# Linear attention ahead of two expert layers: q (k^T v) taken head by head from two row halves

## The chip, the core and the metric

One NeuronCore of a Trainium2 chip runs the whole program. The metric is device time in microseconds (us) of one execution; each figure for the kernel before is from runs of the same program. The engines are named as in the profile: PE (TensorE, matrix products; its weight loads are PEld), ACT (ScalarE), DVE (VectorE), POOL (GpSimd), and SP, whose queue issues most transfers.

## The reference

The inputs are float32: q, k, v of 4 batches x 8 heads x 576 tokens x 64, and the weights of two feed-forward stages.

```python
kv  = einsum('bhsd,bhse->bhde', k, v)
out = einsum('bhsd,bhde->bhse', q, kv)
x   = out / sqrt(mean(out*out, -1) + 1e-6) * g_norm        # RMS norm per token and head
x   = x.transpose(0, 2, 1, 3).reshape(2304, 512)
h   = x @ w_in;  x = (h * clip(h + 3, 0, 6) / 6) @ w_out   # 512 -> 2048 -> 512
p   = domain_probs / (domain_probs.sum(-1) + 1e-9)         # 2304 x 4
out = sum over e of p[:, e] * (relu(x @ w1[e]) @ w2[e])    # 4 experts, 512 -> 1024 -> 512
```

## The kernel before

**Three stages.** The attention stage works through 8 half batches (4 heads each, numbered i). The first feed-forward stage (`ff_in`, `ff_out`) multiplies in three products of split float32 halves. The expert stage does the same in `quad` and `outs`. PE holds 128 x 128 weights at a time; a float32 product appears in the trace as two PE instructions, each with its own weight load, so 10 products are 20 rows' worth of instructions.

**One step of attention.** The loop over i overlaps three half batches: in step i, `att_q(i)` and `att_kv(i)` run, then `att_out(i-1)`, then `att_x(i-2)`.

- `att_q` transposes q by products with the identity (64 x 64 pieces in the four quarters of PE; tile `pq`; the ninth slice goes into the bank `kvp`), and ACT copies the result to `qT` (lines 217 and 219).
- `att_kv` accumulates k^T v for 4 heads, also in quarters (line 229), and ACT copies each head's 64 x 64 block to its place in `kvbd` (line 234, four instructions). `kvbd` holds two heads as a 128 x 128 block-diagonal matrix, zero elsewhere.
- `att_out` multiplies 128 tokens of `qT` with `kvbd` for a pair of heads (line 247): five tiles of tokens (the fifth, odd one has 64 tokens), two pairs of heads, 10 products into three banks `po` (two tiles, two tiles, the odd one). Bank after bank, ACT squares (line 253) and DVE sums over 64 values (line 256).
- `att_rms`: DVE forms mean + 1e-6 (`va`), ACT takes the root (line 279), DVE takes the reciprocal and a Newton step of four instructions (lines 281 to 286), then scales the three banks into `xt` (line 269).
- `att_x` transposes `xt` (line 305) into three banks `px`; ACT scales by g_norm and rounds to the high half (line 315, "hi"), DVE forms the low half (line 316, "lo").

**Order and banks.** PSUM has 8 banks: two for `pq` and `ph`, six (`psb` with 5 and `psc` with 1) for everything else. The order written in the loop is a priority, not the final order: at compile time a planner places each engine's instructions by its own estimate of when they are ready, and may pull later work forward into a gap. On the chip each engine then runs its own list in that fixed order, waiting where it must. So pieces of the weight conversion (`convert`, lines 142 to 160; three ACT and seven DVE instructions for half a weight tile) stand between the steps of attention. The four `ff_in` products that can start early (`EARLY`) are called by `fill()` in the last three steps. The transfers of q, k and v wait in SP's queue for one of seven buffers.

Of the kernel before, what the change touches and what calls it, by code (L numbers as in the profile page):

```python
# [17 lines left out]
def kernel(  # L18
# [63 lines left out]
    psb = ctx.enter_context(tc.tile_pool(name="psb", bufs=5, space=bass.MemoryType.PSUM))  # L82
    psc = ctx.enter_context(tc.tile_pool(name="psc", bufs=1, space=bass.MemoryType.PSUM))

    turn = [0]

    def bank_b(shape, name):
        turn[0] += 1
        pool, tag = (psc, "c") if turn[0] % 6 == 0 else (psb, "b")
        return pool.tile(shape, F32, tag=tag, name=name)  # L90
# [9 lines left out]
    kvbd = [const.tile([P, NP, P], F32, name=f"kvbd{i}") for i in range(2)]  # L100
    ssq = const.tile([P, 5, HH], F32, name="ssq")
# [10 lines left out]
    todo = [(n, h) for n in range(len(ftiles)) for h in range(2)]  # L112

# [16 lines left out]
    def convert(n):  # L130
# [5 lines left out]
        for h in range(2):  # L136
# [24 lines left out]
            load_raw()  # L161
# [7 lines left out]
    def att_load(i):  # L169
        b, hf = divmod(i, 2)  # L170
        t = {}
        for nm, src in (("q", q), ("k", k), ("v", v)):
            m = natile[0] % 7
            natile[0] += 1
            pool, tag = (accp, "acc") if m < 5 else (wp, f"w{m - 1}")
            t[nm] = pool.tile([P, NP, CJ, D], F32, tag=tag, name=f"{nm}in")
            nc.sync.dma_start(
                out=t[nm].rearrange("p r j d -> p r (j d)"),
                in_=src[b, hf * HH:(hf + 1) * HH].rearrange("(r x) (s j) d -> (x s) r (j d)", x=2, j=CJ),
            )  # L180
        st[i] = t
# [6 lines left out]
    def banks(b):  # L188
        c = cut(b)
        w128 = [(o, P) for o in range(0, c - P + 1, P)]  # L190
        rest = c - len(w128) * P
        odd = [(c - rest, rest)] if rest else []
        w128 += [(o, P) for o in range(c, S - P + 1, P)]
        end = c + (S - c) // P * P
        odd += [(end, S - end)] if end < S else []
        assert len(w128) == 4 and odd == [(odd[0][0], D)]
        return [tuple(w128[:2]), tuple(w128[2:]), tuple(odd)]

    half = [slice(x * D, (x + 1) * D) for x in range(2)]

    def att_q(i):

        t = st[i]
        t["qT"] = qTs = wp.tile([P, NP, S], F32, tag=f"w{i % 2}", name="qT")
        qv = qTs.rearrange("p r (s j) -> p r s j", j=CJ)
        pq = [psa.tile([P, CB, CP], F32, tag="a", name="pq") for _ in range(NP)]
        t["kvp"] = kvp = [bank_b([P, 2, D], "kvp") for _ in range(NP)]
        for j in range(CJ):  # L210
            for x in range(2):
                for r in range(NP):
                    to = pq[r][half[x ^ r], j, :] if j < CB else kvp[r][half[x ^ r], 1, :]
                    nc.tensor.matmul(  # L214
                        to, lhsT=t["q"][half[x], r, j, :], rhs=ident[half[x], half[x]], start=True, stop=True)
        for r in range(NP):
            nc.scalar.activation(out=qv[:, r, :, :CB], in_=pq[r].rearrange("p j s -> p s j"), func=AF.Copy)  # L217
        for r in range(NP):
            nc.scalar.activation(out=qv[:, r, :, CB], in_=kvp[r][:, 1, :], func=AF.Copy)

    def att_kv(i):
# [3 lines left out]
        kvp = t["kvp"]  # L225
        for j in range(CJ):
            for x in range(2):
                for r in range(NP):
                    nc.tensor.matmul(  # L229
                        kvp[r][half[x ^ r], 0, :], lhsT=t["k"][half[x], r, j, :], rhs=t["v"][half[x], r, j, :],  # L230
                        start=(j == 0), stop=(j == CJ - 1))
# [5 lines left out]
    def att_out(i):  # L237
# [3 lines left out]
        t["xt"] = xt = wp.tile([P, 3, 2, HH, D], F32, tag=f"w{2 + i % 2}", name="xt")  # L241
        t["po"] = []
        for tt in banks(b):
            po = psb.tile([P, 2, NP, P], F32, tag="b", name="po")
            for m, (o, w) in enumerate(tt):
# [4 lines left out]
            t["po"].append(po)  # L250
        for g, tt in enumerate(banks(b)):
            w, nm = tt[0][1], len(tt)
            nc.scalar.activation(
                out=xt[:w, g, :nm].rearrange("p m h d -> p m (h d)"),
                in_=t["po"][g][:w, :nm].rearrange("p m r e -> p m (r e)"), func=AF.Square)
            nc.vector.tensor_reduce(  # L256
                out=ssq[:w, 2 * g:2 * g + nm, :], in_=xt[:w, g, :nm], axis=AX.X, op=ALU.add)

    def att_rms(i):


        b, hf = divmod(i, 2)
        t = st[i]
        va, r0, w1_, ri = (sp.tile([P, 5, HH], F32, tag=n, name=n) for n in ("va", "r0", "nw", "ri"))

        def scale():
            for g, tt in enumerate(banks(b)):
                w, nm = tt[0][1], len(tt)
                nc.vector.tensor_tensor(
                    out=t["xt"][:w, g, :nm].rearrange("p m h d -> p (m h) d"),  # L270
                    in0=t["po"][g][:w, :nm].rearrange("p m r (h d) -> p (m r h) d", d=D),
                    in1=ri[:w, 2 * g:2 * g + nm, :].rearrange("p m h -> p (m h)").unsqueeze(2).to_broadcast(
                        [w, nm * HH, D]),
                    op=ALU.mult)

        return [
            lambda: nc.vector.tensor_scalar(
                out=va, in0=ssq, scalar1=1.0 / D, scalar2=1e-6, op0=ALU.mult, op1=ALU.add),
            lambda: nc.scalar.activation(out=r0, in_=va, func=AF.Sqrt),
            lambda: nc.vector.reciprocal(out=r0, in_=r0),  # L280
            lambda: nc.vector.scalar_tensor_tensor(
                out=w1_, in0=va, scalar=FMAX, in1=r0, op0=ALU.min, op1=ALU.mult),
            lambda: nc.vector.tensor_tensor(out=w1_, in0=w1_, in1=r0, op=ALU.mult),
            lambda: nc.vector.tensor_scalar(
                out=w1_, in0=w1_, scalar1=-0.5, scalar2=1.5, op0=ALU.mult, op1=ALU.add),
            lambda: nc.vector.tensor_tensor(out=ri, in0=w1_, in1=r0, op=ALU.mult),
            scale,
        ]

    def att_x(i):  # L290

        b, hf = divmod(i, 2)
        t = st.pop(i)
# [483 lines left out]
```

## Time and profile before

| | |
|---|---|
| median of 3 runs | 1234.51 us (1234.01 to 1236.36) |
| the profiled execution, own time | 1233.99 us |
| its span, first to last instruction | 1232.2 us |
| PE busy | 1212.6 us (98%) |
| DVE, ACT busy | 760.4 us, 531.3 us |
| granted PE clock, mean | 0.997 |
| attention's last "lo" (line 316) | starts 98.9 us into the span |

The shares are averages over stages. PE is without a gap from about 73 us to nearly the end; the gaps lie ahead of that, in the attention stage. All of the changed lines act within the first 100 us.

### The profile page before, as it was taken

The page shows a single profiled execution, that of the slowest core. Times are in us where ns is not written, and L with a number is a line of the kernel's source. Part 1 is how long each engine was busy: PE and PEld are TensorE (multiplying, and loading weights), DVE is VectorE, ACT ScalarE, POOL GpSimd, SP SyncE. Part 2 cuts the span into 40 slices and gives each one's busy share as a digit, 9 for nine tenths or more (in the row PEclk, how much of TensorE's full clock was granted, in tenths as well). Part 3 has the DMA queues.
Part 4 walks back from the last instruction along what each step waited for, and adds up shares of the span by engine and source line. Part 5 has one row for each costly group of instructions (what it writes and reads, how often), then busy time and mean ns, then how long its engine had stood idle before and what let it go on. Part 6 is the DMA issues. An engine that isn't in the chain of part 4 may idle for free.

```text
span 1232.2 us, 17425 instructions
## 1 busy us (share of the span) xinstructions
PE 1212.6 (98%) x7069; PEld 1064.8 (86%) x7069; DVE 760.4 (62%) x1457; ACT 531.3 (43%) x1050; POOL 1.6 (0%) x12
## 2 busy tenths in 40 slices
PE   6899999999999999999999999999999999999998
PEld 4778888888888889999999999899989999999997
DVE  6879993783623646565656595656565956565653
ACT  6667642542422434444444454443333533443441
POOL 0000000000000000000000000000000000000000
PEclk8999999999999999999999999999999999999999
DMA  9802320120110002121121131111212322221211
GB/s 357 259 22 71 108 79 1 52 69 1 36 34 1 1 1 69 69 69 69 69 68 66 64 113 60 66 64 67 69 69 69 111 77 69 69 69 69 69 35 52
DMA packets 60832, 87.14 MB, mean 71 GB/s; under 512 B 5200, under 2 KB 37968, under 8 KB 60752
## 3 DMA queue, kind: packets, MB, share of 16 engines
q1 hardware_dynamic: 60592, 86.03, 20.5%
q8 instruction: 55, 0.90, 0.3%
q14 instruction: 25, 0.20, 0.1%
q10 hardware_dynamic: 160, 0.00, 0.0%
HBM read 81.30 MB, written 4.72 MB: 70 GB/s over the span
## 4 chain that ended last, share of the span: by engine, by line
PE 96%; DVE 2%; DMA 1%; ACT 1%; issue 0%; DVEq 0%; ACTq 0%
PE po L636 32%; PE po L357 16%; PE qa L682 14%; PE qb L682 14%; PE ph L334 5%; PE ph L336 5%; PE ph L335 5%; PE po L247 1%; DMA qin<-in_q_dram 1%; PE px L305 1%; DVE ssq L256 0%; PE kvp L229 0%; DVE xl L316 0%; PE pq L214 0%; DMA raw<-in_moe_w_in_dram 0%
## 5 line engine op out<-in xcount | busy, mean ns | idle before, releaser
L636 PE MATMUL po<-wout,g 128*128 128x512 f32 x1728 | 420.3, 392 | 0.0
L636 PEld LDWEIGHTS po<-wout,g 128*128 128x128 f32 x1728 | 322.2, 188 | 61.7
L682 PE MATMUL qa<-xs,win 128*128 128x384 f32 x1008 | 203.9, 337 | 0.0
L682 PE MATMUL qb<-xs,win 128*128 128x384 f32 x1008 | 203.6, 336 | 0.0
L357 PE MATMUL po<-gH,w 128*128 128x512 f32 (+1 forms) x640 | 193.8, 368 | 0.0
L682 PEld LDWEIGHTS qa<-xs,win 128*128 128x128 f32 x1008 | 179.7, 188 | 6.1 <-ACT us L695 0.4
L682 PEld LDWEIGHTS qb<-xs,win 128*128 128x128 f32 x1008 | 179.7, 188 | 5.6
L357 PEld LDWEIGHTS po<-gH,w 128*128 128x128 f32 x640 | 117.1, 188 | 20.0
L341 DVE SCALAR_TENSOR_TENSOR r<-r,ph 128x512 f32<-128x512 f32 (+1 forms) x80 | 50.6, 632 | 111.6 <-ACT r L340 111.4
L334 PE MATMUL ph<-xh,w 128*128 128x512 f32 (+1 forms) x320 | 118.3, 370 | 0.7 <-ACT qT L217 0.7
L335 PE MATMUL ph<-xl,w 128*128 128x512 f32 (+1 forms) x320 | 118.0, 369 | 0.0
L336 PE MATMUL ph<-xh,w 128*128 128x512 f32 (+1 forms) x320 | 118.0, 369 | 0.0
L357 PE MATMUL po<-gL,w 128*128 128x512 f32 (+1 forms) x320 | 117.8, 368 | 0.0
L340 ACT ACTIVATE r<-ph,three 128x512 f32<-128x512 f32 (+1 forms) x80 | 51.4, 643 | 149.1 <-PE ph L336 149.1
L656 DVE SCALAR_TENSOR_TENSOR g<-qa,g 128x384 fp32r<-128x384 f32 x48 | 26.7, 557 | 119.5 <-ACT g L655 118.2
L551 DVE TENSOR_TENSOR wout<-raw,wout 128x512 fp32r<-128x512 f32 x96 | 65.8, 687 | 28.0 <-ACT wout L550 28.0
L656 DVE SCALAR_TENSOR_TENSOR g<-qb,g 128x384 fp32r<-128x384 f32 x48 | 26.8, 557 | 88.6 <-ACT g L655 88.2
L655 ACT ACTIVATE g<-cs 128x384 fp32r<-128x384 f32 x96 | 49.7, 518 | 56.5 <-DVE cs L703 53.4
L550 ACT ACTIVATE wout<-raw 128x512 fp32r<-128x512 f32 x96 | 55.4, 624 | 33.5 <-PE po L636 33.5
L334 PEld LDWEIGHTS ph<-xh,w 128*128 128x128 f32 x320 | 60.3, 188 | 10.9 <-ACT qT L217 0.8
L335 PEld LDWEIGHTS ph<-xl,w 128*128 128x128 f32 x320 | 60.3, 189 | 10.1
L336 PEld LDWEIGHTS ph<-xh,w 128*128 128x128 f32 x320 | 60.3, 188 | 10.1
(93 smaller groups left out, 1249.3 us busy)
## 6 DMA issues: line engine op xcount, KB each, us to landing
raw<-in_moe_w_dram SPq DMA_DIRECT2D x96, 512.0 KB, 4.2
raw<-in_moe_w_in_dram SPq DMA_DIRECT2D x16, 512.0 KB, 3.7
raw<-in_moe_w_out_dram SPq DMA_DIRECT2D x16, 512.0 KB, 3.6
qin<-in_q_dram SPq DMA_DIRECT2D x8, 576.0 KB, 9.7
kin<-in_k_dram SPq DMA_DIRECT2D x8, 576.0 KB, 7.0
vin<-in_v_dram SPq DMA_DIRECT2D x8, 576.0 KB, 7.4
out_dram<-acc SPq DMA_DIRECT2D x18, 256.0 KB, 2.0
dp<-in_moe_domain_probs_dram SPq DMA_DIRECT2D x1, 36.0 KB, 5.0
```

The costliest lines, as they stand in the source:

```text
L334: nc.tensor.matmul(ph, lhsT=w[:, 0, c, :], rhs=xH[t][:, c, :], start=(c == 0), stop=False)
L335: nc.tensor.matmul(ph, lhsT=w[:, 0, c, :], rhs=xL[t][:, c, :], start=False, stop=False)
L336: nc.tensor.matmul(ph, lhsT=w[:, 1, c, :], rhs=xH[t][:, c, :], start=False, stop=(c == KD - 1))
L340: nc.scalar.activation(out=r, in_=ph, func=AF.Relu, bias=three[:, 0:1])
L341: nc.vector.scalar_tensor_tensor(out=r, in0=r, scalar=6.0, in1=ph, op0=ALU.min, op1=ALU.mult)
L357: nc.tensor.matmul(po_t[u, t][o], lhsT=lhsT, rhs=rhs, start=(f == 0 and m == 0), stop=(f == UF[u] - 1 and m == 2))
L550: nc.scalar.activation(out=dst[0], in_=src, func=AF.Copy)
L551: nc.vector.tensor_tensor(out=dst[1], in0=src, in1=dst[0].bitcast(F32), op=ALU.subtract)
L636: nc.tensor.matmul(ps[i], lhsT=lhsT, rhs=w[:, f, y], start=(j == 0 and f == 0 and m == 0), stop=(j == FP - 1 and f == 1 and m == 2))
L655: nc.scalar.activation(out=g[0], in_=src, func=AF.Relu)
L656: nc.vector.scalar_tensor_tensor(out=g[1], in0=src, scalar=0.0, in1=g[0].bitcast(F32), op0=ALU.max, op1=ALU.subtract)
L682: nc.tensor.matmul(bank, lhsT=w[:, wy, AOP[m], c], rhs=xs[m][:, xy, c], start=first and n == 0, stop=n == 5, skip_group_check=True)
```

## The change

- `kvbd` becomes `kvs`: the 64 x 64 blocks of both row halves side by side, 128 x 64 for a pair of heads, with no zeros, copied by two ACT instructions for four (`att_kvc`).
- `att_out` takes each head by itself: 64 rows of `qT` (a row half y) times 64 columns of `kvs`. The four whole tiles give 16 products of 64 x 128 weights and 64 columns, into two banks, one for each row half; the odd tile gives 4 products in the quarters of PE, so that its 64 tokens of both row halves fill all 128 partitions of the third bank. Squares, sums and scalings follow this grouping (`by_head`).
- The sums are 18 values a partition, where they were 20. The root is taken on ACT straight from the sums (scale and bias in the instruction); `va` is formed on DVE beside it; the Newton step is three instructions after the reciprocal.
- `att_x` transposes the whole tiles as before; the odd tile is turned by two products with halves of the identity for each pair of heads.
- The six banks are two pools of three, used three and three in turn. The order in a step is a list, `STEPS`: sums, root and `va`, the transposes, then "hi" and the Newton step; scaling stands ahead of the second and third "lo".
- The early `ff_in` are generators called at two places in a step, from the step of the last half batch on.
- g_norm's load and its root stand ahead of the weight loads; the probabilities' load stands behind the q, k and v of its step, one step later.

```diff
-    psb = ctx.enter_context(tc.tile_pool(name="psb", bufs=5, ...))
-    psc = ctx.enter_context(tc.tile_pool(name="psc", bufs=1, ...))
+    psb = ctx.enter_context(tc.tile_pool(name="psb", bufs=3, ...))
+    psc = ctx.enter_context(tc.tile_pool(name="psc", bufs=3, ...))
...
-        pool, tag = (psc, "c") if turn[0] % 6 == 0 else (psb, "b")
+        pool, tag = (psb, "b") if turn["b"] % 6 < 3 else (psc, "c")
...
-        for r in range(NP):
-            for x in range(2):
-                nc.scalar.activation(
-                    out=kvbd[i % 2][half[x ^ r], r, half[x]], in_=kvp[r][half[x ^ r], 0, :], func=AF.Copy)
+    def att_kvc(i):
+        for r in range(NP):
+            nc.scalar.activation(out=kvs[i % 2][:, r, :], in_=st[i]["kvp"][r][:, 0, :], func=AF.Copy)
...
-                for r in range(NP):
-                    nc.tensor.matmul(
-                        po[:w, m, r, :], lhsT=t["qT"][:, r, o:o + w], rhs=kvbd[i % 2][:, r, :],
-                        start=True, stop=True)
+            po = [bank_b([P, 4, NP, D], "po") for _ in range(2)]
+            for m, o in enumerate(full):
+                for r in range(NP):
+                    for y in range(2):
+                        nc.tensor.matmul(
+                            po[y][:, m, r, :], lhsT=qT[half[y], r, o:o + P], rhs=kv[half[y], r, :],
+                            start=True, stop=True)
...
+            t["po"][2] = po = bank_b([P, NP, D], "po")
+            for r in range(NP):
+                for y in range(2):
+                    nc.tensor.matmul(
+                        po[half[y], r, :], lhsT=qT[half[y], r, odd:odd + D], rhs=kv[half[y], r, :],
+                        start=True, stop=True)
...
+        nc.scalar.activation(out=r0, in_=ssq, func=AF.Sqrt, scale=1.0 / D, bias=eps[:, 0:1])
...
+        nc.vector.reciprocal(out=r0, in_=r0)
+        nc.vector.scalar_tensor_tensor(out=nw, in0=t["va"], scalar=FMAX, in1=r0, op0=ALU.min, op1=ALU.mult)
+        nc.vector.scalar_tensor_tensor(out=nw, in0=nw, scalar=-0.5, in1=r0, op0=ALU.mult, op1=ALU.mult)
+        nc.vector.scalar_tensor_tensor(out=ri, in0=nw, scalar=1.5, in1=r0, op0=ALU.add, op1=ALU.mult)
...
+            if o0 <= odd < o1:
+                for x in range(2):
+                    nc.tensor.matmul(
+                        px[half[x], z, odd - o0:odd - o0 + D], lhsT=t["xt"][:, 4, r, :],
+                        rhs=ident[:, half[x ^ r]], start=True, stop=True)
...
+    STEPS = (
+        ("q", 0), ("qc", 0), ("kv", 0), ("kvc", 0), ("out", 1, 0), ("out", 1, 1),
+        ("sq", 1, 0), ("ssq", 1, 0), ("sq", 1, 1), ("ssq", 1, 1), ("sq", 1, 2), ("ssq", 1, 2),
+        ("rt", 1), ("va", 1), ("x", 2, 0), ("x", 2, 1), ("x", 2, 2), ("hi", 2, 0), ("nw", 1),
+        ("hi", 2, 1), ("hi", 2, 2), ("lo", 2, 0), ("sc", 1, 0), ("sc", 1, 1), ("sc", 1, 2),
+        ("lo", 2, 1), ("lo", 2, 2))
...
         if 1 <= i < NHB - 1:
-            att_load(i + 1)
-        if i == 4:
-            nc.sync.dma_start(out=dp, in_=moe2_domain_probs.rearrange("(t p) e -> p t e", p=P))
+            load(i + 1)
+        if i == 5:
+            load_probabilities()
+        for m, (name, lag, *part) in enumerate(STEPS):
+            if m == 4:
+                conv({0: 6, 1: 11}.get(i, 0))
+            if m in (4, 14) and i >= NHB - 1 and done < len(EARLY):
+                for _ in range(3):
+                    fill(done)
+                done += 1
+            if 0 <= i - lag < NHB:
+                DO[name](i - lag, *part)
```

## Rows read from the trace of the kernel before

**Rows 1.** Whom PE waited for, whole span: us in total, times, longest.
```profile
PE kvp L229 <- ACT qT L219: 4.2, 4, 3.1
PE pq L214 <- DMA qin<-in_q_dram: 3.3, 2, 2.8
PE px L305 <- DVE xl L316: 1.5, 4, 0.5
```

**Rows 2.** Stretch, length, busy PE, PEld, DVE, ACT, POOL, then clock, DMA share, GB/s.
```profile
15.00:46.30 31.30, 25.50 (x678) 21.91 (x678) 27.90 (x68) 20.66 (x55) 0.00 (x0) 0.94 0.92 320
46.30:55.16 8.86, 8.20 (x158) 6.77 (x152) 7.74 (x22) 5.64 (x15) 0.00 (x0) 1.00 0.93 296
...
73.10:97.60 24.50, 24.50 (x135) 19.65 (x136) 19.35 (x44) 16.84 (x35) 0.00 (x0) 1.00 0.07 22
```

**Rows 3.** The chain that ended last, 46.3 to 55 us: start, length, what.
```profile
46.40 2.56 PE po L247 x20
48.96 1.36 PE px L305 x8
...
51.09 0.45 PE px L305 x2
...
51.56 0.47 ACT xh L315
52.04 1.00 ACT qT L217 x2
...
53.27 1.26 PE kvp L229 x36
```

**Rows 4.** PE's weight loads in order of time, 55 to 69 us.
```profile
55.16 2.39 PEld L247 LDWEIGHTS po<-kvbd,qT 128*128 128x128 f32 x20
...
58.20 0.51 PEld L305 LDWEIGHTS px<-ident,xt 64*128 64x128 f32 x4 [0.17 <-DVE ssq L256]
...
62.55 1.25 PEld L229 LDWEIGHTS kvp<-vin,kin 64*64 64x64 f32 x72
...
66.43 0.64 PEld L305 LDWEIGHTS px<-ident,xt 128*128 128x128 f32 x6 [0.17 <-issue]
```

**Rows 5.** DVE's groups by line and shape, 0 to 100 us: busy us, mean ns.
```profile
L256 DVE TENSOR_REDUCE ssq<-xt 128x8 f32<-128x512 f32 x16 | 10.8, 681 | 4.8 <-ACT xt L253 4.4
L269 DVE TENSOR_TENSOR xt<-po,ri 128x512 f32<-128x512 f32 x16 | 10.3, 684 | 0.2
...
L269 DVE TENSOR_TENSOR xt<-po,ri 64x256 f32<-64x256 f32 x8 | 3.2, 406 | 0.0
L256 DVE TENSOR_REDUCE ssq<-xt 64x4 f32<-64x256 f32 x8 | 3.2, 400 | 0.0
...
L316 DVE SCALAR_TENSOR_TENSOR xl<-px,gcol,xh 128x448 fp32r<-128x448 f32 x4 | 2.7, 676 | 0.3 <-ACT xh L315 0.3
L280 DVE RECIPROCAL r<-r 128x20 f32<-128x20 f32 x8 | 2.1, 264 | 0.0
...
L283 DVE TENSOR_TENSOR nw<-nw,r 128x20 f32<-128x20 f32 x8 | 1.4, 174 | 0.1
...
L316 DVE SCALAR_TENSOR_TENSOR xl<-px,gcol,xh 128x128 fp32r<-128x128 f32 x2 | 0.7, 350 | 0.0
```

**Rows 6.** ACT in order of time, near 6 us and 55 to 64 us.
```profile
5.77 1.28 ACT L456 ACT_TABLE_LOAD   x1
...
9.38 1.07 ACT L217 ACTIVATE qT<-pq 128x512 f32<-128x512 f32 x2
...
55.22 0.82 ACT L234 ACTIVATE kvbd<-kvp 64x64 f32<-64x64 f32 x4 [2.00 <-PE kvp L229]
...
57.26 0.96 ACT L253 ACTIVATE xt<-po 128x512 f32<-128x512 f32 x2 [0.17 <-PE po L247]
...
60.34 0.22 ACT L279 ACTIVATE r<-va 128x20 f32<-128x20 f32 x1 [0.51 <-DVE va L277]
...
62.21 0.40 ACT L219 ACTIVATE qT<-kvp 128x64 f32<-128x64 f32 x2
```

More of the change, by code (lines that the diff above doesn't have):

```diff
@@ L112 @@
     todo = [(n, h) for n in range(len(ftiles)) for h in range(2)]
+    ahead = [True]
     def load_raw():
@@ L167, with att_load, tiles @@
     natile = [0]
-    def att_load(i):
+    def att_load(i, nm):
+        if i >= NHB:
+            return
         b, hf = divmod(i, 2)
[L171 to L181, printed above, removed]
+        src = {"q": q, "k": k, "v": v}[nm]
+        m = natile[0] % 7
+        natile[0] += 1
+        pool, tag = (accp, "acc") if m < 5 else (wp, f"w{m - 1}")
+        t = pool.tile([P, NP, CJ, D], F32, tag=tag, name=f"{nm}in")
+        nc.sync.dma_start(
+            out=t.rearrange("p r j d -> p r (j d)"),
+            in_=src[b, hf * HH:(hf + 1) * HH].rearrange("(r x) (s j) d -> (x s) r (j d)", x=2, j=CJ),
+        )
+        st.setdefault(i, {})[nm] = t
     def cut(b):
         return next(o for o, _ in BLK if o > b * S) - b * S
-    def banks(b):
+    def tiles(b):
         c = cut(b)
[L190 to L197, printed above, removed]
+        full = [*range(0, c - P + 1, P), *range(c, S - P + 1, P)]
+        odd = c // P * P if c % P else c + (S - c) // P * P
+        assert len(full) == 4 and sorted([*full, odd]) == sorted({*full, odd}) and S == 4 * P + D
+        return full, odd
     half = [slice(x * D, (x + 1) * D) for x in range(2)]
@@ L237, in att_out, with by_head @@
-    def att_out(i):
+            nc.scalar.activation(out=kvs[i % 2][:, r, :], in_=st[i]["kvp"][r][:, 0, :], func=AF.Copy)
+    def by_head(t, g):
+        if g == 2:
+            return t["xt"][:, 4, :NP, :]
+        return t["xt"][:, :4, 0:4:3, :] if g == 0 else t["xt"][:, :4, 1:3, :]
+    def att_out(i, part):
+        t = st[i]
+        full, odd = tiles(i // 2)
+        if "po" not in t:
+            t["xt"] = wp.tile([P, 5, HH, D], F32, tag=f"w{2 + i % 2}", name="xt")
+            t["po"] = {}
+        qT, kv = t["qT"], kvs[i % 2]
+        if part == 0:
+            po = [bank_b([P, 4, NP, D], "po") for _ in range(2)]
[5 more added lines that the diff above has]
+                            start=True, stop=True)
+            t["po"][0], t["po"][1] = po
+        else:
+            t["po"][2] = po = bank_b([P, NP, D], "po")
[4 more added lines that the diff above has]
+                        start=True, stop=True)
@@ L259, in att_rms @@
[L259 to L288, printed above, removed]
@@ new lines, in att_x @@
+        rs, (o0, o1) = ([y], long) if y < NP else (list(range(NP)), short)
+        px = bank_b([P, len(rs), o1 - o0], "px")
+        full, odd = tiles(b)
+        for z, r in enumerate(rs):
+            for m, o in enumerate(full):
+                if o0 <= o < o1:
+                    nc.tensor.transpose(
+                        px[:, z, o - o0:o - o0 + P],
+                        t["xt"][:, m, 2 * r:2 * r + 2, :].rearrange("p h d -> p (h d)"), ident)
+            if o0 <= odd < o1:
[3 more added lines that the diff above has]
+                        rhs=ident[:, half[x ^ r]], start=True, stop=True)
@@ L378 @@
     EARLY = [(0, t, f) for f in range(UF[0]) for t in range(2)]
-    nearly = [0]
-    def fill():
-        ff_in(*EARLY[nearly[0]])
-        nearly[0] += 1
+    early_in = [ff_in(*x) for x in EARLY]
     def step(n):
         if n < NI and items[n] not in EARLY:
-            ff_in(*items[n])
+            for _ in ff_in(*items[n]):
+                pass
         if n >= LAG:
```

196 lines of the change are left out of this document (99 added, 97 removed).

## The prediction

> **What bounds the kernel now.** I read the page, PE's waits, busy time by stretch, the chain of waits, and then the engines' order of time, in this order. PE is the bound of the whole, at 98% of the span, so a change is worth what it takes from PE's work or from PE's gaps, where PE cannot fill them with something else. Whom PE waited for shows where the gaps are: every wait of note belongs to attention (`kvp`, `pq`, `px`) and none to either feed-forward stage [rows 1]. Busy time by stretch shows the same in order. From 73.1 to 97.6 us PE is busy in all of 24.50 us, although attention's last two half batches still run there, because early `ff_in` work fills in [rows 2]. From there on only PE's own work counts. Ahead of it lie two regimes. From 15 to 46.3 us DVE is busy for 27.90 of 31.30 us: attention and the weight conversion share it, and the chain goes through DVE nearly throughout. From 46.3 us on the conversion is thin, DVE has 7.74 of 8.86 us (some of it for the probabilities), no engine is full, and the chain of waits sets the step.
>
> That chain, for one step [rows 3]: the products `po` start at 46.40, then `px` into two banks; the third `px` waits for the first "lo" and starts at 51.09; "hi" at 51.56; ACT is thereby late for the copies to `qT` (52.04), and `kvp` waits for them (53.27). The next `po` loads start at 55.16 [rows 4]: a step of 8.76 us.
>
> **The change, part by part.**
>
> *The products of q and kv.* Before, 20 weight loads take 2.39 us, 120 ns each [rows 4]. The new whole tiles are 16 products, so 32 loads of 64 rows and 128 columns, each for 64 moving columns where it was 128. No row of before shows two row halves of that width side by side. Below: a 128-column load of `px` takes 0.64 / 6 = 107 ns, and if the halves overlap fully a pair shares that, 53 ns each, 1.71 us. Above: 64 x 128 loads that all stand in the same row half take 0.51 / 4 = 128 ns; if the halves do not overlap, 32 x 128 ns = 4.10 us. The nearest row is `kvp`: 72 loads of 64 x 64 in four quarters take 1.25 us, 17.4 ns each, so one quarter holds 69 ns, and four work at once [rows 4]. Row halves there overlap, so I take half of 120 ns, 60 ns: 32 x 60 = 1.92 us. The odd tile is 8 loads in two quarters, 8 x 35 = 0.28 us.
>
> The Trainium skill ("TensorE: Matmul & The Clock Gate", LDWEIGHTS) says that a load's time goes with its columns and not its rows. By that alone the 32 loads would be 32 x 107 = 3.4 us, 1.5 more than I take. The `kvp` rows agree with the part on columns and show quarters overlapping, but for this shape no run shows it; it is the third rival.
>
> So `po` goes from 2.56 to about 2.2 us. `px` pays some of it back: two 64-row transposes (0.25 us by the 128 ns) become 8 loads of 64 columns in two column halves (0.28 us), and each change of tile shape leaves a gap of 0.17 us in the loads [rows 4], of which I count about three more a step, 0.5 us. PE's own work in a step stays where it was, within 0.2 us. Where PE is full (two steps behind 73.1 us) I therefore take 0, between -0.5 (gaps free) and +3 us (loads one after another).
>
> *Copies, squares and sums.* Four copies to `kvbd` take 0.82 us, two of 128 x 64 take 0.40 [rows 6]: 0.4 us off ACT, in a place where ACT waited 2.00 us for `kvp`; worth nothing by itself. The odd bank's sum, 0.400 us on 64 x 256, becomes 128 x 128: between 0.174 (smallest DVE row) and 0.400, I take 0.27. Its scaling, 0.406, becomes 128 x 128 too: the "lo" of that shape has 0.350, 0.174 below; I take 0.30. The Newton step loses one instruction of 0.174 with its gap, 0.21 [rows 5]. Together DVE loses 0.13 + 0.11 + 0.21 = 0.45 us a step. In the DVE regime (three steps between 15 and 46.3 us) that is 3 x 0.45 = 1.35 us; from 0 (the planner puts conversion there) to 3 us (it also leaves out the conversion that it pulled forward).
>
> *Banks and order.* The third `px` no longer waits for "lo": with six banks in turn, its bank is that of `kvp`, free as soon as ACT has copied it. This cuts the chain of rows 3 at 51.09. The next long way round is: scaling frees the banks of `po`, the next `po` fills them. I sum it from the end of the second scaling: third scaling 0.30; products 1.92 (both banks end together, since each tile writes to both, where before the first bank was done half-way); 0.17 until ACT starts [rows 6]; square 0.60; two sums 1.36, third 0.27; root 0.22 [rows 6]; reciprocal 0.26; Newton 3 x 0.21 = 0.63; one "lo" in between, 0.68; two scalings 1.37. Sum 7.78, and some ten hops at 0.03 make 8.1 us. Against 8.76 that is 0.66 a step, for the three steps from 46.3 us: 2.0 us. Queued on DVE behind a wait for the root are the Newton step and all scalings, and for those the next `kvp` and `po`: it is the same way round, already in the sum.
>
> *Start.* The second table load of ACT (1.28 us at 5.77), the root of g_norm and its two transfers stood in front of the first copy to `qT` at 9.38 [rows 6]. They move to where ACT waits for the first weights. But the next `pq` waits for its transfer anyway, 2.8 us at the longest [rows 1], which covers most of it. I take 0.3 us, between 0 and 1.5.
>
> *Probabilities, early `ff_in`, order of issue.* The load moves one step later, behind other loads; PE waited for no late q, k or v except at the start [rows 1]. The early `ff_in` are the same work, in a stretch where PE is full. Both 0; if the cover were gone the q load behind it would be late by a few us once.
>
> Sum: 0.3 + 1.35 + 2.0 + 0 = 3.65 us. Against the profiled execution's own 1233.99 us that gives 1230.3; the median lies 0.5 us above that execution, so 1230.8 us.
>
> **The rivals.**
>
> *The chain breaks altogether* and a step is as long as PE's own work: `pq` and `kvp` 1.25 each, `po` 2.2, `px` 1.14, eight gaps 1.36, together 7.2 us. Then 8.76 - 7.2 = 1.56 for six steps is 9.4, with the start 9.7 us: 1224.8 us. For it speaks that "hi" no longer blocks ACT and that PE has waits in every step; against it the way round summed above, which needs `po` and its scaling in turn.
>
> *Nothing moves by what can be measured* (0.2%, 2.5 us): the both-banks-at-once end of `po` and conversion put into the gaps eat the 0.66 us, and 1.35 is left: 1233 us. For it speaks that DVE is nearly full up to 46.3 us, and that conversion already stood in the middle of attention's chain.
>
> *Row halves load one after another.* 32 x 107 ns is 1.5 us more a step: in the chain 9.6 us, +0.84 for six steps, 5.0, and 2 x 1.5 where PE is full: 1234.5 + 8.0 - 0.3 = 1242 us. It decides above some 81 ns a load, where 0.66 us are gone. Against it: the 17.4 ns of `kvp`.
>
> "TensorEngine Tiling" in the Trainium skill (Restrictions and Gotchas, PSUM Pressure) says that row tiles may not write to one bank at the same time. The odd tile does that; but so do the quarters of `kvp`, whose rows show four at work.
>
> *`kvp` stands in front of `po`.* Its bank is now freed by scaling, and the list has `kv` ahead of `out`. If the planner keeps that order, the way round holds the copies to `qT` (0.40 and a hop) and `kvp` (1.26) as well: 8.1 + 1.8 = 9.9 us, +1.1 for six steps: 1234.5 + 6.8 - 0.3 = 1241 us. It decides once `kvp` is late by 0.66 us. Against it: the planner fills a gap with what is ready, and `po` needs only the third scaling more.
>
> **How the numbers follow.** Forecast 0.44, the broken chain 0.19, no change 0.18, row halves in turn 0.10, `kvp` in front 0.09. The forecast alone lies between 1228 and 1232.5 us. The range takes in the fast rival and stops a little short of the slow ones: 1223 to 1240. Faster by over 0.2%: 0.44 + 0.19 less 0.03 for the forecast's weak end, 0.60; slower 0.19; within 0.2%: 0.21.
>
> **What would show it.** Right: a step of about 8 us between the starts of `po`; no wait of `px` for "lo"; 32 loads near 60 ns; PE full from about 70 us, 3 to 4 us earlier. Wrong: loads near 107 ns, `kvp` waiting for scaling ahead of `po`, or conversion pulled into every gap so that DVE stays full as long as before. The forecast would be too timid if the steps between 15 and 46 us shrink to 7 us, which would mean that DVE was not the bound there.

## The result, and the profile after

| | before | after |
|---|---|---|
| median on one chip (4 runs before, 3 after) | 1234.43 us | 1249.38 us (1246.15 to 1252.12) |
| the profiled execution: span, granted clock | 1232.2 us, 0.997 | 1247.6 us, 0.989 |
| PE busy, DVE busy | 1212.6 us, 760.4 us | 1232.4 us, 757.3 us |
| first `ph` starts | 70.45 us | 79.16 us |

The ratio is 1.0117, with a 95% interval of 1.0084 to 1.0150: the changed kernel is slower by 15 us, outside the range of 1223 to 1240. A fourth run of the kernel after, 1267.17 us at a granted clock of 0.972, was in a slow state and is left out.

PE waits for little in the kernel after, as before [rows 1]. The third `px` no longer waits for "lo"; one `po` does, for 1.2 us. Whom PE waited for, whole span:

```profile
PE kvp L238 <- ACT qT L229: 4.4, 3, 3.3
PE pq L218 <- DMA qin<-in_q_dram: 2.4, 2, 1.8
PE po L265 <- DVE xl L351: 1.2, 1, 1.2
```

PE is busy 19.8 us longer, so the loss must be PE's own work. Busy time by stretch, of the kernel after (columns as in [rows 2]; the first two lines are the stretches of [rows 2], the rest cuts the first one up):

```profile
15.00:46.30 31.30, 29.39 (x547) 27.21 (x540) 22.88 (x53) 16.50 (x40) 0.00 (x0) 0.61 0.71 264
46.30:55.16 8.86, 8.20 (x226) 7.48 (x227) 6.29 (x17) 4.58 (x14) 0.00 (x0) 1.00 0.85 260
...
15.00:18.00 3.00, 2.11 (x66) 1.80 (x58) 2.87 (x7) 2.40 (x4) 0.00 (x0) 0.50 1.03 404
18.00:21.00 3.00, 3.00 (x46) 2.88 (x50) 2.18 (x4) 1.51 (x4) 0.00 (x0) 0.50 1.05 413
...
27.00:30.00 3.00, 3.00 (x15) 3.00 (x15) 1.43 (x6) 1.34 (x5) 0.00 (x0) 0.50 1.05 399
...
33.00:36.00 3.00, 3.00 (x16) 3.00 (x15) 2.34 (x6) 0.73 (x2) 0.00 (x0) 0.50 0.70 231
36.00:40.00 4.00, 4.00 (x62) 3.32 (x65) 1.97 (x6) 2.71 (x6) 0.00 (x0) 0.54 0.35 137
```

The same view of the kernel before, the stretches in which its clock rose:

```profile
15.00:18.00 3.00, 2.83 (x73) 2.53 (x74) 2.90 (x6) 1.52 (x4) 0.00 (x0) 0.50 1.04 408
18.00:21.00 3.00, 3.00 (x85) 2.81 (x86) 1.16 (x3) 2.09 (x6) 0.00 (x0) 0.91 1.04 411
21.00:24.00 3.00, 1.76 (x39) 1.33 (x37) 2.93 (x7) 2.08 (x8) 0.00 (x0) 1.00 1.06 399
```

Two things are to be seen. The granted clock, third column from the end, goes from 0.50 (1.2 GHz) to 1.00 (2.4 GHz) within 18 to 21 us before; after, it stays at 0.50 until past 39 us, and a figure between the two is a mean over both levels. And where DVE was full (27.90 of 31.30 us, [rows 2]), PE is now full and DVE is not (22.88). In 27 to 30 us and 33 to 36 us PE is busy throughout, with 15 and 16 instructions.

Which instructions take so long, PE in order of time, kernel after, stretches near 27 to 46 us and at 83 us:

```profile
26.87 3.67 PE L265 MATMUL po<-kvs,qT 64*128 64x64 f32 x16
...
32.60 3.67 PE L265 MATMUL po<-kvs,qT 64*128 64x64 f32 x16
...
40.55 2.00 PE L265 MATMUL po<-kvs,qT 64*128 64x64 f32 x16
...
46.17 2.00 PE L265 MATMUL po<-kvs,qT 64*128 64x64 f32 x16
...
83.56 2.00 PE L265 MATMUL po<-kvs,qT 64*128 64x64 f32 x32
```

At 83.56 us a half batch's 32 instructions take 2.00 us, 62.5 ns each, where 60 were forecast and 120 was the price of a whole tile's load [rows 4]. At 40.55 and 46.17 us 16 of them, half as many, take 2.00 us, at the same clock: 125 ns each. At half clock 16 take 3.67 us, 229 ns each. The reason stands in the list that the planner made for PE. The first lines are a half batch as it is written; the others are the next half batch (the number is the place in the list, x8 are eight in a row to one bank):

```
133 L265 MATMUL po_395<-kvs0_110,qT_215 128x64
134 L265 MATMUL po_396<-kvs0_110,qT_215 128x64
135 L265 MATMUL po_395<-kvs0_110,qT_215 128x64
136 L265 MATMUL po_396<-kvs0_110,qT_215 128x64
...
222 L265 MATMUL po_527<-kvs1_111,qT_323 128x64 x8
...
259 L265 MATMUL po_528<-kvs1_111,qT_323 128x64 x8
260 L273 MATMUL po_545<-kvs1_111,qT_323 64x64 x4
```

In the half batches 0, 3, 6 and 7 the two row halves are issued in turn, or nearly so. In 1, 2 and 5 the planner issues all eight products of one row half as soon as their bank is free, and those of the other 25 to 40 places later. Nothing of the other row half then loads beside them. Half batch 4 stands between: its list has six, four and two products of one row half in a row and only the last four in turn, and it takes 3.4 us. PE in order of time, kernel after:

```profile
59.87 2.05 PE L265 MATMUL po<-kvs,qT 64*128 64x64 f32 x20 [1.25 <-DVE xl L351]
...
62.12 0.66 PE L265 MATMUL po<-kvs,qT 64*128 64x64 f32 x6
...
64.99 0.66 PE L265 MATMUL po<-kvs,qT 64*128 64x64 f32 x6
```

A third difference lies where no line was changed, in the first feed-forward stage, from the first `ph` to the last `po`: 413.0 us before (70.5 to 483.5), 421.9 after (79.2 to 501.1). PE's groups by line and shape there, 110 to 480 us (count, busy us, mean ns), kernel after:

```profile
L391 PE MATMUL po<-gH,w 128*128 128x512 f32 x502 | 167.7, 395 | 0.0
...
L366 PE MATMUL ph<-xl,w 128*128 128x512 f32 x232 | 91.6, 395 | 0.0
```

and the kernel before:

```profile
L357 PE MATMUL po<-gH,w 128*128 128x512 f32 x488 | 160.3, 389 | 0.0
...
L335 PE MATMUL ph<-xl,w 128*128 128x512 f32 x228 | 88.8, 390 | 0.0
```

The same product takes 5 to 6 ns longer. What changed for it is where its operands lie: `kvs` is smaller than `kvbd`, so by the shapes of the tiles every later tile on that side of SBUF starts 992 bytes lower. Of the operands of these products that moves the moving ones (`xh`, `xl`, `gH`, `gL`); the weights `w` come from a pool on the other side and stay.

Fourth, the probabilities. The planner put their first sum between attention's instructions. Whom DVE waited for, 0 to 110 us, and the chain of waits around it, kernel after:

```profile
DVE psum_e L498 <- DMA dp<-in_moe_domain_probs_dram: 3.6, 1, 3.6
```

```profile
52.03 5.55 DMA dp<-in_moe_domain_probs_dram
57.59 0.02 issue
57.61 0.24 DVE psum_e L498
```

### The profile page after: what moved, and what is told of

It is laid out like the page before. It is cut to its first block, busy times and chain, and to the rows that moved or that the text cites. A ratio compares the mean times of both kernels' runs of the same rounds, so it can differ in the third digit from the quotient of the medians.

```text
span 1247.6 us, 17805 instructions
## 1 busy us (share of the span) xinstructions
PE 1232.4 (99%) x7277; PEld 1080.6 (87%) x7277; DVE 757.3 (61%) x1449; ACT 525.2 (42%) x1033; POOL 1.1 (0%) x10
## 4 chain that ended last, share of the span: by engine, by line
PE 97%; DMA 2%; DVE 0%; ACT 0%; issue 0%
PE po L679 31%; PE po L391 16%; PE qb L725 14%; PE qa L725 14%; PE ph L365 5%; PE ph L367 5%; PE ph L366 5%; PE po L265 2%; PE kvp L238 1%; DMA qin<-in_q_dram 1%; PE px L332 1%; PE pq L218 1%; DMA dp<-in_moe_domain_probs_dram 0%; DMA raw<-in_moe_w_in_dram 0%; PE px L337 0%; PE po L273 0%
## 5 line engine op out<-in xcount | busy, mean ns | idle before, releaser
L679 PE MATMUL po<-wout,g 128*128 128x512 f32 x1728 | 415.4, 389 | 0.0
L391 PEld LDWEIGHTS po<-gL,w 128*128 128x128 f32 x320 | 60.0, 188 | 11.6
```

Of the source, the lines that this page charges most:

```text
L391: nc.tensor.matmul(po_t[u, t][o], lhsT=lhsT, rhs=rhs, start=(f == 0 and m == 0), stop=(f == UF[u] - 1 and m == 2))
L679: nc.tensor.matmul(ps[i], lhsT=lhsT, rhs=w[:, f, y], start=(j == 0 and f == 0 and m == 0), stop=(j == FP - 1 and f == 1 and m == 2))
```

## The experiments

Five theories are named by letters. S: the start addresses in SBUF slow the feed-forward stage. C: products in row halves leave PE's granted clock low for longer. D: the wait for the probabilities costs its 3.6 us. U: row halves that are not issued in turn are added PE work. T: row halves cost time wherever they stand. U was formed only after the eighth to tenth run, so the expectations before those do not have it. Ratios are to the kernel before, run on the same chip, with 95% intervals; its medians there lay between 1233.99 and 1235.10 us.

**Start addresses alone.** A pad tile at the left of SBUF is made 992 bytes longer in the kernel after, so that later tiles lie where they lay before; in the second run it is made 32 bytes longer in the kernel before. Each engine's list is otherwise the same.

```diff
-    PADL, PADR = 48, 248
+    PADL, PADR = 296, 248      # kernel after
-    PADL, PADR = 48, 248
+    PADL, PADR = 56, 248       # kernel before
```

> The changed kernel with one number changed: the pad ahead of the left-hand tiles of SBUF is 296 floats instead of 48, so that these tiles (x, g, the sums) start 992 bytes higher, by my count where they stood before the change. Every instruction list stays the same. Theory S (the start of the moving operands decides the pace of the first feed-forward stage): twelve products po take 2.72 us again instead of 2.80, and the time falls by 8 to 12 us to about 1240 us. Rival B (the two pools of three banks slow that stage): 2.80 us and about 1250 us as before this edit.

> The kernel before with the same pad 8 floats (32 bytes) longer and nothing else. Theory S: twelve products po take 2.80 us instead of 2.72 and the time rises by 8 to 12 us, to about 1244 us. Rival B: nothing changes, 1234.5 us.

Measured: the kernel after with the pad 1243.28 us, 1.0071 [1.0056, 1.0086]; the kernel before with the shift 1242.72 us, 1.0069 [1.0054, 1.0084]. PE's groups as above, 110 to 480 us, first the kernel after with the pad, then the kernel before with the shift:

```profile
L391 PE MATMUL po<-gH,w 128*128 128x512 f32 x507 | 166.3, 389 | 0.0
...
L391 PE MATMUL po<-gH,w 128*128 128x256 f32 x96 | 19.2, 283 | 0.0
```

```profile
L357 PE MATMUL po<-gH,w 128*128 128x512 f32 x495 | 165.5, 395 | 0.0
...
L357 PE MATMUL po<-gH,w 128*128 128x256 f32 x86 | 16.8, 279 | 0.0
```

The product of 512 columns follows the address both ways, 389 ns and 395; that of 256 columns goes the other way, 283 and 279. Some 1,450 of the former at 5.5 ns are 8 us, less 1 for some 280 of the latter. With the pad the first feed-forward stage takes 413.6 us (79.2 to 492.8) for 421.9, 8.3 less. The expert stage gives 2.2 of it back: from its first `po` to its last it takes 742.3 us with the pad (495.0 to 1237.3) and 740.1 without (503.3 to 1243.4). What is left is 6.1 us, by spans (1247.6 to 1241.5) as by medians. The kernel before with the shift lost 8.7 us, but its mean granted clock was lower too, 0.9915 against 0.9941 in the kernel before beside it. S is shown, at some 6 us. About 9 us of loss stay, and all further kernels have their tiles where the kernel before has them.

**Three attempts to lift the clock or take the wait away.** From the padded kernel: three products of full 128 x 128 weights and 512 columns behind the first `kv`; the probabilities' load one step earlier; one full product of 384 columns more in every step. The added products' results are not used.

```diff
+            if name == "kvc" and i == 0:
+                wb = bank_a([P, TB], "wb")
+                for _ in range(3):
+                    nc.tensor.matmul(wb, lhsT=st[0]["qT"][:, 0, :P], rhs=st[0]["qT"][:, 0, :TB], start=True, stop=True)
...
+        if i == 4:
+            load_probabilities()
...
+            nc.tensor.matmul(full_bank[:, P:], lhsT=qT[:, 0, :P], rhs=qT[:, 0, :TB - P], start=True, stop=True)
```

> The kernel of e1 with three added float32 products of 128 x 128 weights and 512 columns behind the first k^T v, whose result nobody reads. Theory C (in the changed kernel the granted clock of PE is 0.50 from 15 to 39 us and products in row halves run at that): the full array products bring the clock up, it reads near 1.00 from about 17 us, the last k^T v ends near 74 us instead of 81, and the time is 5 to 8 us below e1. Rival (DVE and the order of the steps are what limits attention there, as my prediction had it): the clock may rise, but the last k^T v ends within 2 us of 81 and the time is within 2 us of e1.

> The kernel of e1 with the load of the probabilities back at its former place, one step earlier and ahead of that step's q, k and v. Theory D (DVE's wait for the probabilities, 3.6 us at 57.6 us in the changed kernel, lies on the path): that wait is gone and the time is 2 to 4 us below e1. Rival (DVE would have waited for ACT's squares there anyway): under 1 us below e1.

> The kernel of e1 with one float32 product of 128 x 128 weights and 384 columns in every step of attention, ahead of the odd tile's products, into the unused part of their bank; nobody reads it. It costs PE about 0.65 us a step, 5 us in all. Theory C (at the lower clock only because its products in row halves and quarters leave much of PE unused, the stage is slow for that): the clock stays at 1.00 for more of 15 to 39 us, the first ph comes at 77 us or earlier (79.2 in e1) in spite of the added work. Rival C2 (the clock falls in the waits for the first transfers and comes back when it will, whatever the products): the clock reads 0.50 as long as in e1 and the time rises by some 5 us.

Measured: 1247.06 us, 1.0104 [1.0083, 1.0126]; 1241.91 us, 1.0059 [1.0043, 1.0076], single runs from 1236.72 to 1248.28; 1252.80 us, 1.0124 [1.0088, 1.0160]. With three products at the start the clock was at 0.99 to 1.00 from 15 to 24 us, fell back to 0.50 for 27 to 36 us, and the time grew by 3.8 us, which neither of its two expectations had. With a product more in each step it stayed at 0.50 until 44 us, although these were full products, and the time grew by 9.5 us, where C2 had 5. Full products as such do not settle it, and the load alone is lost in the spread that the clock makes: the run of 1236.72 us had a mean clock of 0.993, that of 1248.28, which is the one in the trace, 0.981. None of the three says more.

**Whole tiles back.** From the padded kernel, the 16 products in row halves become 8 of 128 x 128 with the block-diagonal `kvbd`; sums, root, Newton step, banks, order and the odd tile stay as changed. The second run also loads the probabilities at the fourth step, ahead of its q, k and v.

```diff
-                    for y in range(2):
-                        nc.tensor.matmul(
-                            po[y][:, m, r, :], lhsT=qT[half[y], r, o:o + P], rhs=kv[half[y], r, :],
-                            start=True, stop=True)
+                    nc.tensor.matmul(
+                        po[m // 2][:, m % 2, r, :], lhsT=qT[:, r, o:o + P], rhs=kv[:, r, :],
+                        start=True, stop=True)
...
+        if i == 3:
+            load_probabilities()
```

> The kernel of e1 with the product of the whole tiles put back: block-diagonal weights of 128 rows, 8 products of 128 x 128 x 128 in place of 16 in row halves, four copies to kvbd in place of two, banks by tile; the pad is chosen so that the left-hand tiles start where they did. Everything else of the change stays. Theory C: the clock is back at 1.00 by about 20 us as in the kernel before, the first ph comes 5 to 9 us earlier than in e1 (79.2), and the time is 1234 to 1238 us. Rival C2 (the order of steps, the banks or the start are what costs attention its 8.7 us): the first ph stays within 2 us of 79 and the time within 2 us of 1243.

> The kernel of e6 with the load of the probabilities two steps earlier, ahead of the loads of step 3. Theory D: DVE's wait for it (3.65 us in the changed kernel) is gone and the first ph comes 2 to 4 us earlier than in e6; if both theories hold this version is the first below the kernel before, 1230 to 1234 us. Rival: within 1 us of e6, because the step was waiting for something else as well.

Measured: 1234.55 us, 1.0000 [0.9990, 1.0010], and 1234.12 us, 0.9994 [0.9984, 1.0003]. The row halves hold all that was lost in attention. Busy time by stretch of the second kernel:

```profile
18.00:21.00 3.00, 3.00 (x68) 2.77 (x70) 2.24 (x5) 1.69 (x5) 0.00 (x0) 0.50 1.03 408
21.00:24.00 3.00, 2.47 (x65) 2.11 (x59) 2.90 (x7) 2.18 (x8) 0.00 (x0) 0.92 1.07 400
```

The wait for the probabilities (1.6 us in the first of the two) is gone in the second, for 0.4 us of median, as the rival had it, and the intervals do not tell that from nothing: if D holds, it is small. And whole tiles at full clock, PE in order of time of the second kernel, take what row halves in turn take:

```profile
85.44 1.95 PE L266 MATMUL po<-kvbd,qT 128*128 128x128 f32 x16
```

**Row halves late, early, and with all rows.** All from the kernel just told. In the first, half batches 4 to 7 have row halves; in the second, 0 to 3. The third has the 16 products in all half batches, each with all 128 rows of weights, against `kvbd`'s 64 columns of one head, in which the other rows are zero, so it adds work.

```diff
+            t["by_row"] = i >= 4      # second: i < 4; third: True
...
+                        nc.tensor.matmul(
+                            po[y][:, m, r, :], lhsT=qT[half[y], r, o:o + P], rhs=kv[half[y], r, half[y ^ r]],
+                            start=True, stop=True)
...
# third
+                            po[y][:, m, r, :], lhsT=qT[:, r, o:o + P], rhs=kv[:, r, half[y ^ r]],
```

> The kernel of the experiment before this one (whole-tile products, probabilities loaded early), with products in row halves from the fifth half batch on alone. Theory C (row halves cost time only through the clock, while the clock is still low): the clock rises at about 21 us as there, and the time is 1232.5 to 1234.5 us: the products of four steps take 2.00 us where whole tiles take 2.4, of which at most 1.6 us in all is seen. Rival T (row halves cost time by themselves, by their banks that end together, wherever they stand): 4 of the 8.6 us that whole tiles gave back are lost again, 1238 us or more.

> The counterpart: products in row halves in the first four half batches alone, whole tiles in the last four. Theory C: granted clock 0.50 until past 33 us, first product ph some 6 to 9 us late, 1240 to 1244 us. Rival T: half of the loss, about 1238 us, with the clock as with whole tiles.

> The same 16 products by head, in the same banks and order as in the changed kernel, but each with all 128 rows as weights, and the other head's 64 rows of the moving columns zero (extra work: products with zeros). Per step 32 loads of about 120 ns, 3.8 us where row halves take 2.0. Theory C in the form that it is the half-filled rows which leave the clock low: it rises at about 21 to 24 us in spite of 64 moving columns, and what is lost then is PE work, up to 1.4 us a step, 1237 to 1245 us. Rival C2 (it is the short moving columns, the banks or the order): 0.50 until past 33 us and 1245 us or more.

Measured: late 1237.32 us, 1.0016 [1.0007, 1.0026]; early 1239.49 us, 1.0048 [1.0030, 1.0066]; all rows 1243.69 us, 1.0076 [1.0059, 1.0093]. Busy time by stretch, the early kernel and then the one with all rows:

```profile
27.00:30.00 3.00, 3.00 (x15) 3.00 (x16) 2.83 (x9) 1.94 (x6) 0.00 (x0) 0.50 1.09 303
...
40.00:46.00 6.00, 5.71 (x76) 5.29 (x72) 3.87 (x11) 2.14 (x5) 0.00 (x0) 0.50 0.01 3
```

```profile
21.00:24.00 3.00, 3.00 (x79) 2.81 (x79) 1.77 (x4) 1.18 (x5) 0.00 (x0) 0.60 1.07 400
24.00:27.00 3.00, 3.00 (x95) 2.86 (x95) 1.05 (x3) 1.67 (x6) 0.00 (x0) 1.00 1.03 408
```

The early kernel's ten runs fall in two groups: six at a mean clock of 0.988 to 0.990 took 1237.03 to 1239.81 us, four at 0.981 and 0.982 took 1243.80 to 1245.54. So within one kernel some 6 us hang on 0.008 of the mean clock, which is about 19 us more at half clock. The trace is of the run of 1245.54 us, where the clock stayed at 0.50 until 59 us. C's forecast lies between the groups; T's, with the clock as with whole tiles, does not fit.

With all rows, and the same number of products, columns and banks, the clock rose at 23 us. Ahead of the rise only the rows filled were different, and with them the time of the products that were in turn (16 instructions in 3.67 us at half clock, where row halves in turn take about 2); the 64 moving columns, the banks and the order were not, and the rival C2 of this expectation falls. The longer time alone does not lift the clock: in the kernel after, 16 instructions of 64 rows take the same 3.67 us at 26.87 and 32.60 us, and it stays at 0.50. The products with all rows in order of time, half batch 0 at its first 16 instructions, half batch 1, and one in turn:

```profile
17.83 3.67 PE L270 MATMUL po<-kvbd,qT 128*128 128x64 f32 x16
...
26.86 2.00 PE L270 MATMUL po<-kvbd,qT 128*128 128x64 f32 x16
...
51.06 3.79 PE L270 MATMUL po<-kvbd,qT 128*128 128x64 f32 x32 [0.16 <-DVE xt L334]
```

With 128 rows, 16 instructions take 2.00 us and 32 take 3.79, whatever their order. So 16 of 64 rows in 2.00 us is the time of loads that share nothing. The late kernel fits neither C nor T as they stood: it lost 3.2 us against whole tiles, in the chain of waits, 40 to 76 us, at

```profile
63.66 1.94 PE po L270 x16
...
68.70 1.93 PE po L270 x16
```

Both are half batch 5, one row half and then the other: this is what led to theory U.

**In turn by force.** The padded kernel with one tile of two banks for both row halves, so that all 16 products become ready together (the other tiles share four banks); the second run loads the probabilities early.

```diff
-            po = [bank_b([P, 4, NP, D], "po") for _ in range(2)]
+            both = pse.tile([P, 2, 4, NP, D], F32, tag="e", name="po")
+            po = [both[:, y] for y in range(2)]
```

> The changed kernel with the first experiment's addresses, and one PSUM tile of two banks for both row halves, so that the planner can only issue the 16 products of a half batch together, the two row halves in turn (before, it issued the 8 of one row half and later the 8 of the other in the half batches 1, 2 and 5). Theory U (the loss in attention is PE work: row halves that are not in turn load one after another, 8 products in 2.00 us at full clock and 3.67 at half): 32 loads in 2.00 us everywhere at full clock, PE work less by 3.7 us in the half batch at low clock and by 2.0 in each of the two others; 1243.3 less 5 to 7.7 gives 1235.5 to 1238 us. Rival C (row halves leave the clock low, in turn or not): granted clock 0.50 until past 33 us again, and 1240 to 1243 us.

> The same with the probabilities loaded early, two steps before, ahead of that step's q, k and v. Both theories: 0 to 3.6 us less than the kernel beside it, by the wait of DVE for that transfer; by theory U the products are then as the prediction took them, and if its chain holds too the time comes below that of before, 1231 to 1236 us; by rival C 1237 to 1243 us.

Measured: 1240.35 us, 1.0041 [1.0028, 1.0054], single runs from 1234.96 to 1242.72; 1240.09 us, 1.0048 [1.0033, 1.0062]. All half batches are now issued in turn; PE in order of time, half batch 1, in the first kernel at full clock and in the second at half:

```profile
30.71 2.00 PE L270 MATMUL po<-kvs,qT 64*128 64x64 f32 x32
```

```profile
31.38 3.68 PE L270 MATMUL po<-kvs,qT 64*128 64x64 f32 x32
```

Three of the nine us came back, fewer than U alone gives. In the traces the clock was at 0.50 until 27 us in the first kernel (the run of 1234.96 us) and until past 39 us in the second; and with four banks in place of six for the rest, `kvp` waits for "lo" (4.6 us in the first). So this kernel holds C and a new wait together. Its ten runs part by the clock: the three at 0.989 or above, which is the mean clock of the padded kernel (0.989, 1243.28 us), took 1234.96 to 1238.03 us, about what U gives; the seven at 0.982 to 0.986 took 1239.82 to 1242.72.

**U and C apart, with the banks as they were.** Row halves in half batches 4, 6 and 7 (in turn, clock up); then in 0, 3, 4, 6 and 7 (all that are in turn), run twice; then in 0 alone.

```diff
+            t["by_row"] = i in (4, 6, 7)     # then: i not in (1, 2, 5); then: i == 0
```

> The kernel with row halves from the fifth half batch on (1237.3 us), but with whole tiles in the sixth as well, where its list had the two row halves one behind the other. Theory U (only row halves that are not issued in turn cost time): the 2.0 us of that half batch at least come back, 1234 to 1235.3 us, level with whole tiles everywhere (1234.1). Rival T (row halves cost time wherever they stand): 1236.5 us or more.

> Row halves in the half batches 0, 3, 4, 6 and 7, where the planner issues them in turn, whole tiles in 1, 2 and 5, where it does not. Theory U alone: all of the added PE work is gone, clock up by 24 us as with whole tiles, 1234 to 1235.5 us. Theory C beside it (row halves leave the clock low even in turn): the products of half batch 0 between 17 and 24 us keep the granted clock at 0.50 until 27 us or later, and 1236 to 1240 us.

> The kernel of the run before, again, for its trace (its median was 1237.4 us, 3.3 above whole tiles everywhere). Theory C beside U: granted clock 0.50 from about 13 to 27 us or later, where whole tiles everywhere rose at 21. Theory U alone: up by 24 us, and the 3.3 us must show in waits.

> Row halves in the first half batch alone, in turn (8 products at about 18 us, 8 at about 22 us), whole tiles in all others. Theory C: the clock rises some 3 to 6 us later than with whole tiles everywhere, and the time is 1235 to 1237.5 us. Theory U alone: 1233.5 to 1235 us, level with whole tiles.

Measured: 1234.91 us, 0.9999 [0.9989, 1.0009]; 1237.38 us, 1.0021 [1.0009, 1.0033]; again 1236.99 us, 1.0016 [1.0006, 1.0026]; the first half batch alone 1236.22 us, 1.0011 [1.0002, 1.0021]. Late row halves in turn cost nothing: T falls, and U is shown for half batch 5, since whole tiles in the one half batch that was not in turn took back the late kernel's loss (2.4 us of 3.2, where the added products are 2.0). For the half batches 1 and 2 it is argued from the same durations. Busy time by stretch, row halves in half batch 0 alone:

```profile
21.00:24.00 3.00, 3.00 (x49) 2.77 (x45) 1.39 (x4) 1.75 (x7) 0.00 (x0) 0.50 1.07 400
24.00:27.00 3.00, 3.00 (x77) 2.79 (x72) 3.00 (x8) 1.72 (x5) 0.00 (x0) 0.66 1.03 408
```

The clock rises at 26 us here, at 27 in the kernel beside it, at 21 with whole tiles everywhere. Single traces vary in this: in the six with whole tiles in half batch 0, two of them of the kernel before and its shifted version, the clock rises at 18 to 24 us, in nine with row halves there at 26 to 59 us (the kernel with full products at the start and the first trace of the second kernel here are not counted). The mean clocks over all runs agree: 0.9934 to 0.9940 with whole tiles everywhere or late row halves, 0.9911 to 0.9915 in the three runs here with row halves in half batch 0. So C holds, for row halves in turn as well, at about 2 us for the first half batch (2.1 against whole tiles everywhere, 1.3 against the late row halves on the same chip).

## Why the prediction was wrong, step by step

The rungs, by medians:

| kernel | median, us | step, us |
|---|---|---|
| after | 1249.38 | |
| start addresses as before | 1243.28 | -6.1 |
| whole tiles in half batches 1, 2, 5; probabilities early | 1236.99 | -6.3 |
| whole tiles in 3, 4, 6, 7 too | 1236.22 | -0.8 |
| whole tiles in 0 too | 1234.12 | -2.1 |

The runs come from several chips and spread by 1 to 6 us, so the steps are good to about 1 us; by the ratios to the kernel before on the same chip they are 5.7, 6.8, 0.6 and 2.1.

*The step that failed: 32 loads at 60 ns, "PE's own work in a step stays where it was, within 0.2 us".* The price per load was right where the row halves are in turn (62.5 ns), and so was the upper bound where they are not (64 x 128 loads in one row half 128 ns; measured 125). The rival "row halves load one after another" came nearest, with 107 ns a load and the turning point at 81, but had it in every half batch. What I did not do is ask whether the planner would leave the order as written. Each row half has its own bank, the banks come free one after the other, and the account of the kernel before says that the planner pulls forward what is ready. Of the three half batches out of turn, two paid 4.0 us instead of 2.0 at full clock, and one 7.3 instead of 3.7 at half; half batch 4, partly in turn, paid 3.4. The Trainium skill ("TensorEngine Tiling (Array Packing)", Key Properties) says that different tiles can load and multiply in parallel. The trace agrees, 62.5 ns against 125, but only for neighbours in the list.

*The clock had no term.* The prediction took 15 to 46.3 us as bound by DVE, at full clock. After, PE ran at half clock there for some 20 us longer in the traces and was the bound, so DVE's savings had little to act on. The profiled run of the kernel before had the clock up early, at 0.997 in the mean, where its runs beside the experiments have 0.994 in the middle. The savings were sized rightly: the odd tile's scaling was forecast at 0.30 us and its sum at 0.27 [rows 5]. DVE's groups by line and shape, 0 to 110 us, kernel after:

```profile
L318 DVE TENSOR_TENSOR xt<-po,ri 128x128 f32<-128x128 f32 x8 | 2.2, 281 | 0.0
L289 DVE TENSOR_REDUCE ssq<-xt 128x2 f32<-128x128 f32 x8 | 2.2, 277 | 0.0
```

The Trainium skill ("TensorE: Matmul & The Clock Gate", Part 1) says that the clock starts throttled and that activity releases it. In the view by stretch of the kernel after, PE is busy in all of 18 to 36 us at 0.50, so a busy PE in this view was not enough to foresee it. U and C may feed each other, since products that last longer at half clock put off what comes behind them; the 6.3 us rung holds both, and no run parts them there. An estimate: at 6 us for 0.008 of mean clock, as in the early kernel, the padded kernel's 0.989 against 0.9936 with whole tiles makes C 3 to 4 of its 9 us and leaves 5 to 6 for U.

*Start addresses* were not costed. They are 6 of the 15 us, in stages in which no instruction changed, and no rival had them.

*Probabilities*, taken at 0: a DVE wait of 3.6 us on the chain, whose removal gave 0.4 us (1234.55 to 1234.12), and 1.4 and 0.3 in two pairs that spread more, none of it clear of noise. The planner had moved their reader into attention, which the prediction did not look at.

*Start*, 0.3 us: none. The table load is gone from its place, but the first copy to `qT` starts at 9.89 us instead of 9.38 [rows 6], behind the same copy for the weights as before, which now waits 3.10 us for DVE where it waited 1.58. Where the table load stood, ACT now waits. ACT in order of time, kernel after, then the copy in the kernel before:

```profile
9.35 0.63 ACT L164 ACTIVATE w<-r 128x512 fp32r<-128x512 f32 x1 [3.10 <-DVE r L162]
9.89 1.07 ACT L227 ACTIVATE qT<-pq 128x512 f32<-128x512 f32 x2
```

```profile
8.85 0.63 ACT L158 ACTIVATE w<-r 128x512 fp32r<-128x512 f32 x1 [1.58 <-DVE r L156]
```

*The chain, 2.0 us.* The wait of the third `px` for "lo" is gone, as forecast. Yet with whole tiles, right addresses and early probabilities, everything else that was forecast to gain leaves 0.9994 [0.9984, 1.0003]: at most 2 us, not 3.65. Nor do row halves help PE at full clock, 2.00 us where 8 whole tiles take 1.95; the 2.2 us for `po` should have been 2.4. In the trace of that kernel with whole tiles the clock rose about 3 us later than in the trace of the kernel before and was 0.78 and 0.65 in 30 to 36 us, but that does not account for the missing gain: the mean clock of its ten runs, 0.9936, is that of the 19 runs of the kernel before beside them, 0.9934. What the sum of the chain left out stays open. Open too is what exactly lifts the clock: three full products at the start had it up at 15 us but not for long, and one more in every step had it up no earlier.

## What to carry to other kernels

A pair of row halves is worth its price only while the two stand next to each other in PE's list: where a planner orders the instructions, look at what makes each half ready (here two banks that came free one after the other), and give both one condition. Read the granted clock by stretch before counting an early stretch as bound by another engine, and be wary of half-filled products in the stretch in which it rises: here row halves in the first half batch alone cost 1 to 2 us. Compare the mean clocks of all runs, and not of the one trace alone. When a tile changes its size, everything behind it in SBUF moves: compare the mean time of an untouched product in both kernels before looking for the loss in the changed lines.

## What was not expected of the hardware

- A float32 product of 128 x 128 weights and 512 columns took 389 or 395 ns with the same instructions, by a shift of 32 or of 992 bytes of SBUF tiles; one of 256 columns 283 or 279, the other way round. Over the first feed-forward stage this is 8.3 us, of which the expert stage gives back 2.2. In the first stage only the moving operands had moved. Both shifts are odd multiples of 32 bytes; no other shift was tried.
- PE was busy throughout 18 to 36 us and the granted clock stayed at 0.50 while half batches of 64-row products ran; with 128 rows in the same products it rose at 23 us.
- At full clock, 16 instructions of 64 x 128 weights in one row half take 2.00 us, as do 16 of 128 x 128 with 64 columns; 32 in two row halves in turn also take 2.00 us.
